# Chunk totals of a gated linear attention: from one-column matmuls to a small DMA, in a new program order

## Chip, cores and metric

One core of a Trainium2 chip. The metric is the device time of one launch in microseconds. Each version is run several times beside the kernel before on the same chip. A profile is one execution; its span is some 2 us shorter than the device time.

## The reference

A gated linear attention (4 batches, 8 heads, 768 steps, head size 48), then a feed-forward layer on its output (384 to 2048 to 384) with the gate `h * cos(h)`.

```python
for t in range(S):
    state = alpha[:, :, t, :, None] * state + np.einsum('bhd,bhe->bhde', k[:, :, t], v[:, :, t])
    y[:, :, t] = np.einsum('bhd,bhde->bhe', q[:, :, t], state)
...
h = x @ w_in
g = h * np.cos(h)
return (g @ w_out).astype(np.float32)
```

## The kernel before

Each sequence is cut into 6 chunks of 128 steps, 24 chunks in all. Per chunk, ScalarE takes the logarithm of alpha; a matmul with a triangle of ones sums it over time (positions on partitions, 8 x 48 = 384 columns); ScalarE takes `exp` of the sum and of its negative. q and k are multiplied by these, so that inside the chunk the attention is a masked product of two matrices. The state passed to the next chunk is scaled by the chunk's total decay. That total is the last row of `exp(cumsum)`, but it is needed down the partitions (one number per row of the state), so it has to be turned from a row into columns.

The kernel before computes it again in the other direction, with one-column matmuls:

```python
def cums(j0, n):                                   # chunks j0 .. j0+n-1, n = 1 or 2
    ...
    for i in range(lo, lo + n):
        nc.tensor.matmul(cum_ps[g][:, i, 0:HD], triu_bf, lnab[:, g % 2, i, :, 0:D], start=True, stop=True)
        for p in range(NP):                        # 4 pairs of heads
            nc.tensor.matmul(cum_ps[g][:, i, HD + p : HD + p + 1],
                lnab[:, g % 2, i, 2 * p : 2 * p + 2].rearrange("s h d -> s (h d)"), ones_bf, ...)

def exps(j0, n):
    ...                                            # icp: exp(-cumsum)
    nc.scalar.activation(out=cp_t[g][:, lo : lo + n], in_=cum_ps[g][:, lo : lo + n, 0:CW], func=AF.Exp, scale=1.0)

def emask(j):                                      # GpSimd: total x block mask, used when the state is scaled
    ...
```

The whole program is a list of small units in a string `ORDER`, run in that order on each engine. `F`, `G` are halves of the first feed-forward product, `V`, `W` of the second, `f_`, `g_` the cosine on ScalarE, `p`, `Q_` the gate on VectorE, `C`/`E` cumsum and exponentials of a pair of chunks, `w3` three dummy matmuls that are meant to keep TensorE's clock up.

## Time and profile before

| | before |
|---|---|
| time, median of the first runs | 192.87 us |
| first feed-forward matmul | 32.9 us after the start |
| from there to the last TensorE work ("the middle") | 154.4 us |
| ScalarE busy | 119.4 us of 190.7 |

The prediction shows the lines. TensorE is the bound; from 33 us on it has no pause to speak of, and before that, waits between engines decide.

### The profile page before, as it was taken

To read this page: it belongs to the slowest core of one execution; us is meant where nothing else is said; L and a number is where in the kernel's file an instruction comes from. 1 tells how busy PE (TensorE), PEld (TensorE's weight loads), DVE (VectorE), ACT (ScalarE), POOL (GpSimd) and SP (SyncE) were. 2 spreads that over 40 slices of the span, in tenths; PEclk is the share of its full clock that TensorE was granted. 3 is DMA by queue.
4 is the path that set the end of the run, shared out by engine and by line. 5 is a ranking of instruction groups with operands and counts; after the bars stand their busy time and mean duration, and the time that the engine had idled before them with its cause. 6 is when DMAs were issued, how large, how long until landed. Compare 5 with 4: busy or idle time off the path is not lost.

```text
span 190.7 us, 5672 instructions
## 1 busy us (share of the span) xinstructions
PE 181.7 (95%) x2410; PEld 138.3 (73%) x2410; DVE 128.3 (67%) x159; ACT 119.4 (63%) x135; POOL 74.8 (39%) x116
## 2 busy tenths in 40 slices
PE   0999999999999999999999999999899999999992
PEld 0345545998766887696987788968669877797761
DVE  6137458999686389649577886885667685578520
ACT  3211448799555859984974999887586363364522
POOL 3422763212923550853961747064450456010000
PEclk9999999999999999999999999999999999999999
DMA  6999999999999989899999779996956798321112
GB/s 129 188 186 187 163 286 364 343 370 213 214 225 225 215 161 228 182 198 194 235 188 170 170 120 194 182 196 142 168 134 140 154 205 168 87 64 24 41 45 83
DMA packets 123225, 34.22 MB, mean 179 GB/s; under 512 B 116544, under 2 KB 121664, under 8 KB 123200
## 3 DMA queue, kind: packets, MB, share of 16 engines
q1 hardware_dynamic: 119744, 29.14, 82.3%
q10 hardware_dynamic: 3456, 4.72, 7.4%
q8 instruction: 19, 0.31, 0.7%
q14 instruction: 6, 0.05, 0.1%
HBM read 25.17 MB, written 4.72 MB: 157 GB/s over the span
## 4 chain that ended last, share of the span: by engine, by line
PE 90%; DMA 5%; DVE 1%; SPq 1%; ACT 1%; issue 0%; DVEq 0%; ACTq 0%
PE t L330 33%; PE o_new L352 31%; PE w_new L368 8%; PE t L235 4%; PE t L218 3%; DMA t<-kqb 3%; PE t L292 2%; PE cum_new L157 2%; PE t L260 2%; PE t L289 2%; PE t L313 2%; DMA a_new<-in_alpha_dram 2%; PE cum_new L161 1%; DVE t L244 1%; SPq L104 1%
## 5 line engine op out<-in xcount | busy, mean ns | idle before, releaser
L330 PE MATMUL t<-x,w 128*128 128x128 bf16 x1152 | 70.4, 219 | 0.0
L352 PE MATMUL o_new<-w,g_new 128*128 128x384 bf16 x384 | 68.8, 326 | 0.0
L344 DVE TENSOR_TENSOR g_new<-t,c_sb 128x1024 bf16<-128x1024 f32 x48 | 57.8, 1218 | 15.0 <-ACT c_sb L338 14.6
L330 PEld LDWEIGHTS <-w 128*128 128x128 bf16 x1152 | 65.6, 98 | 1.5
L338 ACT ACTIVATE c_sb<-t,halfpi 128x1024 bf16<-128x1024 f32 x48 | 52.4, 1113 | 18.8 <-PE t L330 15.9
L352 PEld LDWEIGHTS <-g_new 128*128 128x128 bf16 x384 | 35.4, 98 | 20.2
L185 POOL TENSOR_TENSOR kqb<-t,icp_new 128x384 bf16<-128x384 f32 x24 | 23.9, 999 | 19.0 <-ACT icp_new L175 10.6
L244 DVE TENSOR_TENSOR t<-t,mask_f 128x1024 bf16<-128x1024 f32 x24 | 29.0, 1216 | 3.1 <-PE t L235 3.1
L274 POOL TENSOR_TENSOR ub<-sc,Em 128x384 bf16<-128x384 f32 x16 | 13.3, 830 | 37.8 <-DVE sc L272 36.1
L357 ACT ACTIVATE o_sb<-o_new 128x384 f32<-128x384 f32 x24 | 11.7, 489 | 25.9 <-PE o_new L352 25.9
L191 POOL TENSOR_TENSOR kqb<-t,cp_new 128x384 bf16<-128x384 f32 x22 | 21.9, 1000 | 12.0 <-DMA t<-in_q_dram 10.7
L299 DVE CAST t<-t 128x384 bf16<-128x384 f32 x24 | 13.3, 554 | 12.6 <-PE t L292 12.6
L195 POOL CAST vpb<-t 128x384 bf16<-128x384 f32 x24 | 12.4, 519 | 19.1 <-DMA t<-in_v_dram 16.5
L368 PE MATMUL w_new<-warm 128*128 128x512 bf16 x67 | 19.7, 426 | 0.0
L175 ACT ACTIVATE icp_new<-cum_new 128x768 f32<-128x768 f32 (+1 forms) x13 | 9.8, 758 | 15.4 <-PE cum_new L161 14.8
L224 DVE COPY t<-t 128x1024 bf16<-128x1024 bf16 x13 | 8.9, 688 | 10.0 <-PE t L218 9.9
L144 ACT ACTIVATE lnab<-a_new 128x768 bf16<-128x768 f32 (+1 forms) x13 | 10.3, 795 | 5.4 <-DMA a_new<-in_alpha_dram 4.8
L137 ACT ACT_TABLE_LOAD x9 | 11.5, 1283 | 2.4 <-ACT o_sb L357 1.6
L338 ACT ACT_TABLE_LOAD x9 | 11.5, 1283 | 0.6 <-ACT o_sb L357 0.5
L272 DVE TENSOR_TENSOR sc<-t,ub 128x384 f32<-128x384 f32 x16 | 8.9, 554 | 4.5 <-PE t L260 4.4
L292 PE MATMUL t<-vpb,t 128*128 128x48 bf16 x192 | 11.3, 183 | 0.2 <-DVE t L244 0.2
L157 PE MATMUL cum_new<-lnab,triu_bf 128*128 128x384 bf16 x24 | 7.3, 333 | 4.3 <-ACT lnab L144 4.3
(43 smaller groups left out, 132.0 us busy)
## 6 DMA issues: line engine op xcount, KB each, us to landing
a_new<-in_alpha_dram SPq DMA_DIRECT2D x24, 192.0 KB, 4.6
t<-in_q_dram SPq DMA_DIRECT2D x24, 192.0 KB, 4.4
t<-in_v_dram SPq DMA_DIRECT2D x24, 192.0 KB, 4.5
t<-in_k_dram SPq DMA_DIRECT2D x24, 192.0 KB, 4.8
out_dram<-o_sb ACTq DMA_DIRECT2D x24, 192.0 KB, 3.1
w1f<-in_moe_w_in_dram SPq DMA_DIRECT2D x4, 768.0 KB, 7.9
w2f<-in_moe_w_out_dram SPq DMA_DIRECT2D x4, 768.0 KB, 10.7
t<-kqb SPq DMA_TRANSPOSE x11, 4.0
```

The lines of the kernel that those rows point to most:

```text
L185: nc.gpsimd.tensor_tensor(out=khb[:, j % 3, :, 0:D], in0=k_t.pop(j), in1=icp.rearrange("s (h d) -> s h d", h=H), op=ALU.mult)
L191: eng.tensor_tensor(out=qhb[:, j % 3, :, 0:D], in0=q_t.pop(j), in1=cp[:, 0:HD].rearrange("s (h d) -> s h d", h=H), op=ALU.mult)
L195: nc.gpsimd.tensor_copy(out=vpb[:, j % 3, :, 0:D], in_=v_t.pop(j))
L244: nc.vector.tensor_tensor(out=t.rearrange("s (h t) -> s h t", h=H), in0=A_ps.pop(j).rearrange("s (h t) -> s h t", h=H), in1=mask_f.unsquee ...
L274: eng.tensor_tensor(out=ub[:, us(j), :, 0:96].rearrange("r p (a e) -> r p a e", a=2), in0=sc.rearrange("r p (a e) -> r p a e", a=2), in1=E ...
L292: nc.tensor.matmul(t[:, h * D : (h + 1) * D], A_t[j][:, ACOL[h] * C : (ACOL[h] + 1) * C], vpb[:, j % 3, h], start=first, stop=True, skip_g ...
L299: nc.vector.tensor_copy(out=t, in_=y_ps.pop(j)[:, 0:HD])
L330: nc.tensor.matmul(t[:, f], w1[:, kk, ft * C : (ft + 1) * C], x_t[j][:, kk], start=(kk == 0), stop=(kk == 2))
L338: nc.scalar.activation(out=c_sb, in_=h_ps[j, half], func=AF.Sin, bias=halfpi, scale=1.0)
L344: nc.vector.tensor_tensor(out=g_new, in0=h_ps.pop((j, half)), in1=c_t.pop((j, half)), op=ALU.mult)
L352: nc.tensor.matmul(o_ps[j][:, 0:DM], g[:, f], w2[:, half * HF + f], start=(f == 0 and half == 0), stop=(f == HF - 1 and half == 1))
L368: nc.tensor.matmul(w_ps, warm[:, 0:C], warm, start=True, stop=True)
```

## The change

Its intent: take 96 matmuls from TensorE, the bound, and let the DMA engines turn the row into columns. The exponential is written in another layout, so that the 8 values for one partition stand side by side; two DMAs of 48 rows per pair of chunks spread the last row. The program order was made anew for it.

```diff
-            for p in range(NP):
-                nc.tensor.matmul(
-                    cum_ps[g][:, i, HD + p : HD + p + 1],
-                    lnab[:, g % 2, i, 2 * p : 2 * p + 2].rearrange("s h d -> s (h d)"),
-                    ones_bf, start=True, stop=True,
-                )
...
-            cp_new = cpool.tile([C, 2, CW], FP, tag="cpl")
+            cp_new = cpool.tile([C, 2 * D, 2, NP], FP, tag="cpl")
...
-        nc.scalar.activation(out=cp_t[g][:, lo : lo + n], in_=cum_ps[g][:, lo : lo + n, 0:CW],
-                             func=AF.Exp, scale=1.0)
+        nc.scalar.activation(
+            out=cp_t[g][:, :, lo : lo + n].rearrange("s x i p -> s i p x"),
+            in_=cum_ps[g][:, lo : lo + n, 0:HD].rearrange("s i (p x) -> s i p x", p=NP),
+            func=AF.Exp, scale=1.0)
+        for a in range(2):
+            nc.scalar.dma_start(
+                out=tot[64 * a : 64 * a + D, g % 4, lo : lo + n],
+                in_=cp_t[g][C - 1 : C, a * D : (a + 1) * D, lo : lo + n])
...
     ORDER = (   # all of it replaced
```

In the write of the exponential the innermost index is x, whose step in `cp` is 2 x 4 floats, 32 bytes. The q product reads `cp` with the same step.

## The prediction

> **What bounds the kernel now.** I read the page from the top: busy shares, slices, the chain, then the groups by form, and last the stretches and the timeline.
>
> ```profile
> span 190.7 us, 5672 instructions
> PE 181.7 (95%) x2410; PEld 138.3 (73%) x2410; DVE 128.3 (67%) x159; ACT 119.4 (63%) x135; POOL 74.8 (39%) x116
> ...
> PE   0999999999999999999999999999899999999992
> ...
> PE 90%; DMA 5%; DVE 1%; SPq 1%; ACT 1%; issue 0%; DVEq 0%; ACTq 0%
> ```
>
> TensorE is busy in every slice but the first and the last, and the chain is TensorE for 90%. Busy does not mean useful, though: 67 of its instructions are dummy 512-column matmuls (group L368, 19.7 us) that keep its clock up while the start-up waits for others. So I split the span at the first feed-forward matmul. The chain view has that at 32.97 us and the last TensorE work ending at 187.33. The three stretches:
>
> ```profile
> 0.00:33.00 33.00, 28.15 (x246) 14.03 (x247) 17.90 (x31) 13.13 (x19) 14.35 (x29) 1.00 1.17 213
> 33.00:187.40 154.40, 153.55 (x2166) 124.27 (x2165) 110.44 (x129) 105.81 (x117) 60.43 (x87) 1.00 0.86 174
> 187.40:190.70 3.30, 0.00 (x0) 0.00 (x0) 0.00 (x0) 0.42 (x1) 0.00 (x0) 1.00 0.33 119
> ```
>
> The columns after the length are TensorE, weight loads, VectorE, ScalarE and GpSimd. In the middle TensorE lacks under 1 us of being always busy. Since ends of matmuls are modelled, I check it by start-to-start time: the chain shows 24 feed-forward-1 matmuls in 1.34 us, 8 feed-forward-2 matmuls in 1.30, 8 scores in 0.33, the state in 0.28, outputs in 0.36 (0.22 for a first chunk), eight transposes in 0.45, three in 0.18, cumsum with totals 0.27 per chunk. What stands after the first feed-forward matmul is then 48 x 1.34 + 48 x 1.30 = 126.7, scores 19 x 0.33 = 6.3, outputs 18 x 0.36 + 3 x 0.22 = 7.1, states 16 x 0.28 = 4.5, transposes 8 x 0.45 + 10 x 0.18 = 5.4, cumsums 16 x 0.27 = 4.3: 154.3 us against 154.4 measured. There is no slack to win in the middle. It gets shorter only if TensorE has less to do. The first 33 us are the other place: there waits decide, and dummies fill.
>
> **What the Trainium skill says.** "TensorE: Matmul & The Clock Gate", section "Wait — 56ns, not 53.3ns?", gives a floor of about 25 ns start to start however few columns a matmul has. The trace agrees, and shows what one column costs:
>
> ```profile
> 18.47 0.33 PE L157 MATMUL cum_new<-lnab,triu_bf 128*128 128x384 bf16 x1
> 18.63 0.24 PE L161 MATMUL cum_new<-ones_bf,lnab 128*128 128x1 bf16 x4
> 18.74 0.32 PE L157 MATMUL cum_new<-lnab,triu_bf 128*128 128x384 bf16 x1
> ...
> L161 PE MATMUL cum_new<-ones_bf,lnab 128*128 128x1 bf16 x96 | 5.8, 164 | 0.0
> ```
>
> The four stand between 18.63 and 18.74: 0.11 us per chunk, 27 ns each. The mean of 164 ns in the group's row is latency, and its 5.8 us is not what they cost.
>
> The same page, section "What's actually happening", says that the array starts at half clock and needs some 3.4 us of sustained work. The trace agrees in kind: the first 19 dummies take 6.89 us (0.36 each), later ones 0.215. "GPSIMD Engine Reference", section 7 "Performance pitfalls for Q7 kernels", says that reads with a step over 8 bytes cost about 50% more per element; no row of the kernel before reads so, but the changed one will. [...]the quickest output store of this trace landed in 1.9.
>
> **The change, part by part.** (1) Removed: 96 one-column matmuls, 24 x 0.11 = 2.6 us of TensorE. Eight chunks' worth (0.9 us) lies in the start-up, where dummies and waits absorb it. Sixteen chunks (C4 to C11 in pairs) lie in the middle, where it counts in full: 16 x 0.11 = 1.76 us. (2) Removed: the 0.91 us clearing of lnab on VectorE; nothing at the start waits for it. (3) Removed on GpSimd: eight or nine small Em products (12 of two chunks each instead of 20), 0.22 us each, beside other work.
>
> (4) Added: 26 small DMAs on ScalarE's queue.
>
> ```profile
> L358 ACTq DMA_DIRECT2D out_dram<-o_sb x24: 338/338/406, 49.7 to 187.9; - x24
> L191 POOL TENSOR_TENSOR kqb<-t,cp_new 128x384 bf16<-128x384 f32 x22 | 21.9, 1000 | 12.0 <-DMA t<-in_q_dram 10.7 <-ACT cp_new L177 1.2
> ```
>
> An issue holds that queue 0.34 us, so 26 x 0.34 = 8.8 us, 0.7 per exponential pair. ScalarE goes from 119 to about 128 busy-or-issuing of 190: not the bound. In the start-up, though, each pair of issues stands ahead of the next logarithm. I estimate 0.3 to 0.6 us on the path there. In the middle the tot tile is needed many microseconds after the exponential, so 2 to 4 us of landing are hidden. (5) Changed layout: cp is now written and read with 32-byte steps. If the page's 50% holds, the 22 products of row L191 go from 1.0 to 1.5 us, GpSimd from 75 to about 84 us, 44%: hidden in the middle, and at most one product (0.5 us) on the start-up path. I take the strided exponential as unchanged at 0.81 us; no row shows it.
>
> (6) Moved: the whole order. Before the first feed-forward matmul the new order has 64 dummies (67 before), the same transposes, scores and outputs, and three states instead of four. After it stand the fourth state (+0.28) and 5 dummies (+1.08). So the middle has 154.4 - 1.76 + 0.28 + 1.08 = 154.0 us of work: only 0.4 less.
>
> For the start-up I walked the new order by hand with the durations above (eviction of transposes 0.69, masking 1.21, state sum and output cast 0.56, weight cast 0.68, products 1.0). The loads go out one after another at about 1.0 us as before; the alpha of chunk 0 is now second, so its logarithm starts about 0.6 us later. 9 and 4 cold dummies bring the first transposes to about 11.3 us (11.45 before); the pair of transposes for chunk 1 falls near 15.7, the second cumsum pair near 19, output 0 near 19.5. From there single buffers in PSUM tie TensorE to VectorE: transposes 2 at about 21, state 1 at 23.7, output 1 at 24.9, output 2 at 27.4, transposes 4 at about 28.8 (behind the q and k products on GpSimd), their eviction 30.3, the x copy 31.4, state 2, and the first feed-forward matmul at about 31.8. That is 1.2 us earlier than 32.97, give or take 1.2.
>
> Just after it the order runs three feed-forward halves in a row; the fourth needs the third and fourth quarter of w1, and I find VectorE's last cast ending near 38.5 behind two gates, with TensorE there from about 37.6. I charge 0.4 us for this and for seams like it. The sum: -1.2 (start) - 0.4 (middle) + 0.4 (waits) = -1.2 us on 192.87: about 191.7 us.
>
> **The rivals.** A: the start-up gain is not there. Slower q products and DMA issues ahead of logarithms push the first feed-forward matmul to 33 us or beyond. For it: the chain in the start-up alternates between engines, so each delay adds. Then 193 to 194. B: ScalarE stalls on completion marks. In the built program the eight completion marks of DMAs are used in turn, and 24 of the 26 small DMAs first wait for an earlier DMA to land, as the loads and stores do too. A load held up behind a transpose on SyncE's queue, or a load that now waits for a small DMA, could stop ScalarE and with it the feed-forward buffers. For it: SyncE's queue waits for others 7.6 and 7.3 us in the wait table. Against: the stores had the same waits, and TensorE lost nothing. If it bites several times, 195. C: the new order packs better than I walked, with the first feed-forward matmul at 30 and no later wait: -3 - 0.4, 189.5; a bit more would need an even shorter start. D: the full 2.6 us shows and the dummies cover real waits that vanish: 190.2.
>
> **Range and chances.** Faster by over 2% needs under 189.0, 3.9 us: more than all removed matmuls together, so only the start-up could give it. Slower needs over 196.7, which takes repeated stalls under B. Start-up uncertainty of about 1.5 us and middle waits of -0.4 to +3 give 189.0 to 194.5 for 8 in 10. Chances: faster 0.13, same 0.80, slower 0.07.
>
> **What would show it.** Right: row L161 gone; TensorE busy down some 2 us with 69 dummies; the first feed-forward matmul at 31 to 33 us; q products on GpSimd near 1.5 us; small-DMA issues near 0.34 us each; the middle at 153.5 to 155.5 us. Wrong: first feed-forward matmul before 30.5 or after 34; slices of TensorE below 9 in the middle; long waits of ScalarE's queue for DMAs; exponentials much above 0.81 us.

## More of the kernel before

One more detail matters later: how ScalarE passes through the end of an exponential pair. In the timeline (start, length, engine, line, operation, output and input) of the kernel before:

```profile
63.53 0.81 ACT L177 ACTIVATE cp_new<-cum_new 128x776 f32<-128x776 f32 x1
64.36 1.28 ACT L338 ACT_TABLE_LOAD   x1
65.66 1.11 ACT L338 ACTIVATE c_sb<-t,halfpi 128x1024 bf16<-128x1024 f32 x1
```

The exponential ends, and the switch to the cosine's table begins at once: 0.83 us from the start of the one to the start of the other.

## The result

198.01 us against 192.61 for the kernel before in the same runs: ratio 1.028 (95% interval 1.023 to 1.034). It is slower by more than 2%, and outside the range. (Ratios are the mean of one kernel's fast runs over the mean of the other's in the same rounds, so not quite the quotient of the medians quoted.)

From the page of the kernel after:

```profile
span 196.0 us, 5512 instructions
PE 180.3 (92%) x2312; PEld 136.2 (70%) x2316; DVE 127.1 (65%) x158; ACT 128.1 (65%) x135; POOL 77.1 (39%) x108
...
PE   1996999999998989999999999899899999799993
...
PE 13%; ACT 2%; issue 1%; ACTq 1%; DVE 0%; DVEq 0%
```

TensorE's slices now have 8s and a 7 in the middle. The chain, TensorE for 90% before, can be followed back for 18% of the span only; then it reaches ScalarE's queue, where instructions were issued and no recorded wait is left to follow. The stretch from the first feed-forward matmul (32.15 us) to TensorE's end:

```profile
32.15:192.79 160.64, 154.81 (x2114) 123.43 (x2112) 110.84 (x130) 111.42 (x116) 64.55 (x84) 1.00 0.79 167
```

160.6 us for which 154.0 were predicted, and TensorE idle for 160.64 - 154.81 = 5.8 us of them. The start is near what was predicted (31.8). ScalarE's groups and the record of the tot tile, then the timeline of ScalarE at the end of a pair:

```profile
L169 ACT ACTIVATE cp_new<-cum_new 128x768 f32<-128x768 f32 x11 | 17.3, 1569 | 0.0
L135 ACT ACT_TABLE_LOAD x9 | 11.5, 1283 | 2.4 <-ACT o_sb L354 1.6 <-PEq L427 0.7
L335 ACT ACT_TABLE_LOAD x9 | 11.5, 1283 | 7.3 <-DVE t L241 1.7 <-DVE x L315 1.6 <-POOL kqb L188 1.3
```

```profile
L174 ACTq DMA_DIRECT2D tot<-cp_new x26: 508/588/1232, 7.0 to 161.1; - x26
```

```profile
117.89 1.57 ACT L169 ACTIVATE cp_new<-cum_new 128x768 f32<-128x768 f32 x1
119.49 1.17 ACTq L174 DMA_DIRECT2D tot<-cp_new  x2
120.74 1.28 ACT L335 ACT_TABLE_LOAD   x1 [1.28 <-DVE t L241]
```

The exponential takes 1.57 us, not 0.81; each DMA issue holds ScalarE's queue for 0.59 us (median; minimum and maximum beside it), not 0.34. From the exponential's start to the table load is 2.85 us, against 0.83. The table loads' "idle before" rose from 0.6 to 7.3 us, and the names of its releasers are of no use: those engines had long been done. ScalarE was issuing DMAs, which do not count as busy. So its busy 128 us understate it: 9.1 us of longer exponentials are in it, but not the 26 issues, which fill 16.5 us of the timeline. Here is how that reaches TensorE, late in the run. First come pieces from the beginning of the chain that ended last (start, length, what), then the timeline behind them:

```profile
160.54 0.53 ACTq L174
...
161.10 0.60 ACTq L174
...
161.79 0.08 ACT L335
...
163.09 1.11 ACT c_sb L335
164.20 0.39 ACT o_sb L354
...
164.63 2.76 PE o_new L349 x16
167.39 1.35 PE t L327 x24
```

```profile
168.77 1.11 ACT L335 ACTIVATE c_sb<-t,halfpi 128x1024 bf16<-128x1024 f32 x1 [0.85 <-PE t L327]
...
169.92 1.22 DVE L341 TENSOR_TENSOR g_new<-t,c_sb 128x1024 bf16<-128x1024 f32 x1 [1.35 <-ACT c_sb L335]
...
171.06 0.55 DVE L269 TENSOR_TENSOR sc<-t,ub 128x384 f32<-128x384 f32 x1
...
171.63 0.40 PE L232 MATMUL t<-t 48*128 48x128 bf16 x8 [1.26 <-DVE sc L269]
```

The chain begins at the two DMA issues of the last pair. Behind them stand the table load, a cosine and the copy of an output (`o_sb`); TensorE's second product starts late for that copy (0.30 us), and the first product and the next cosine (168.77) follow it. That late cosine makes the gate late, the gate stands on VectorE ahead of the state sum, and the second of two groups of scores on TensorE waits 1.26 us. In e12 below, with the same order and a shorter hold, the same two groups run in one piece:

```profile
163.47 0.62 PE L231 MATMUL t<-t 48*128 48x128 bf16 x16
```

### The profile page after: what moved, and what is told of

The parts are those of the page before. It is cut to its first block, busy times and chain, and to the rows that moved or that the text cites. A ratio compares the mean times of both kernels' runs of the same rounds, so it can differ in the third digit from the quotient of the medians.

```text
span 196.0 us, 5512 instructions
## 1 busy us (share of the span) xinstructions
PE 180.3 (92%) x2312; PEld 136.2 (70%) x2316; DVE 127.1 (65%) x158; ACT 128.1 (65%) x135; POOL 77.1 (39%) x108
## 5 line engine op out<-in xcount | busy, mean ns | idle before, releaser
L349 PEld LDWEIGHTS <-g_new 128*128 128x128 bf16 x384 | 36.0, 98 | 21.3 <-issue 0.4
L188 POOL TENSOR_TENSOR kqb<-t,cp_new 128x384 bf16<-128x384 f32 x22 | 26.0, 1187 | 12.3 <-DMA t<-in_q_dram 8.0
L365 PE MATMUL w_new<-warm 128*128 128x512 bf16 x65 | 19.2, 420 | 1.4 <-DVE warm L57 1.2
L169 ACT ACTIVATE cp_new<-cum_new 128x768 f32<-128x768 f32 (+1 forms) x13 | 19.0, 1460 | 0.0
L365 PEld LDWEIGHTS <-warm 128*128 128x128 bf16 x69 | 6.6, 105 | 11.5 <-issue 6.6
```

What stands on the lines that cost most here:

```text
L169: nc.scalar.activation(out=cp_t[g][:, :, lo : lo + n].rearrange("s x i p -> s i p x"), in_=cum_ps[g][:, lo : lo + n, 0:HD].rearrange("s i ...
L188: eng.tensor_tensor(out=qhb[:, j % 3, :, 0:D].rearrange("s (p a) d -> s p a d", a=2), in0=q_t.pop(j).rearrange("s (p a) d -> s p a d", a=2 ...
L349: nc.tensor.matmul(o_ps[j][:, 0:DM], g[:, f], w2[:, half * HF + f], start=(f == 0 and half == 0), stop=(f == HF - 1 and half == 1))
L365: nc.tensor.matmul(w_ps, warm[:, 0:C], warm, start=True, stop=True)
```

## The experiments

Theory 1: the changed arithmetic holds ScalarE too long (stepped exponential, DMA issues), and everything behind it in order comes late. Theory 2: the new program order packs TensorE worse by itself. Theory 3: the small DMAs act in another way, by their landing or by the completion marks that they share with the loads.

| version | time, us | ratio (95%) | first ff matmul | middle | TensorE idle in it |
|---|---|---|---|---|---|
| before | 192.2 to 192.6 | 1 | 32.9 | 154.4 | 0.8 |
| after | 198.01 | 1.028 (1.023 to 1.034) | 32.15 | 160.6 | 5.8 |
| order alone | 192.64 | 1.003 (1.001 to 1.004) | 30.2 | 158.1 | 2.8 |
| arithmetic alone | 208.67 | 1.084 (1.079 to 1.090) | 33.3 | 170.5 | 11.4 |
| after, contiguous exponential* | 191.87 | 1.000 (0.996 to 1.005) | 31.75 | 156.7 | 2.8 |
| after, no small DMAs* | 190.76 | 0.991 (0.989 to 0.993) | 31.3 | 155.1 | 2.0 |
| after, neither* | 188.21 | 0.982 (0.977 to 0.986) | 29.4 | 153.5 | 0.4 |
| neither, ScalarE copy of 1.9 us per pair* | 193.38 | 1.005 (1.000 to 1.010) | 31.25 | 157.0 | 2.5 |
| no small DMAs, ScalarE copy of 1.4 us* | 196.60 | 1.021 (1.017 to 1.026) | 32.0 | 159.4 | 5.0 |
| one DMA in place of two | 192.83 | 1.005 (1.000 to 1.009) | 32.1 | 156.6 | 2.9 |
| one DMA, steps moved to the read | 190.42 | 0.989 (0.985 to 0.994) | 30.9 | 154.0 | 0.9 |

Starred versions give a wrong result on purpose. Times are medians of fast runs. The last three columns come from each version's one profile: the start of its first feed-forward matmul, the stretch from there to the end of the last one, and TensorE's idle time in that stretch. (For "order alone" the profile is a second, single run; see below. e6 and e7, which failed, are told in the text.)

### Order alone, arithmetic alone

```diff
 # e1: before, with the new ORDER
-        "E_": emask,
+        "E_": lambda g: (emask(2 * g), emask(2 * g + 1)),
 # e2: after, with the old ORDER; emask again per chunk, from tot
+            out=Em, in0=tot[:, (j // 2) % 4, j % 2].unsqueeze(2).to_broadcast([C, NP, 2]),
```

> The old arithmetic (four one-column matmuls per chunk, no small DMA, contiguous exponential) in the new program order. Theory 1 (ScalarE is made late by the added work: the exponential at 1.57 us in place of 0.81, and 26 DMA issues of 0.59 us): the new order without that work has no long gaps on TensorE; first feed-forward matmul at or before 32 us, time 190 to 193.5 us. Theory 2 (the new order itself packs worse on TensorE, whatever the arithmetic): 196 to 199 us, with the gaps near 62, 72, 124, 138 and 171 us still there.

> The new arithmetic (small DMAs, strided exponential, no one-column matmuls) in the old program order. Theory 1: the same 24 us of extra ScalarE time meet an order that made no room for them: 196 to 201 us. Theory 2: the old order keeps TensorE packed and the removed matmuls show as up to 1.8 us: 190 to 192.5 us.

192.64 and 208.67 us. The order alone is as fast as before (0.3% apart), so theory 2 falls. It starts the feed-forward part at 30.2 us, 2.7 us earlier than before, and its middle is 3.7 us longer in the single run that was profiled. The new arithmetic in the old order is slower by 8%, more than the 196 to 201 us that theory 1 gave: in the new order the same arithmetic costs 10.7 us less (208.67 - 198.01). But not all of that loss need be ScalarE's. In the old order GpSimd's product with the totals (`Em`) stands close behind the exponentials, and GpSimd stood there for the small DMAs to land:

```profile
POOL Em L197 <- DMA tot<-cp_new: 28.2, 8, 7.3
```

That is 28.2 us in 8 waits, against 9.1 us in two in the kernel after. So the landing, which the prediction called hidden, shows on GpSimd in another order; what it cost TensorE there, no run separates. In that profile the granted clock was 0.973 as well, so a little of the loss is clock.

The first profile of the order-only kernel fell in an execution at half the TensorE speed: 370.85 us, with TensorE 97% busy and the first feed-forward product 141.9 us in its group's row in place of 70.4. (The granted clock that the record gives for it is 1.00 all the same.) Its three timed runs were normal. The profile was taken again:

> The order-only kernel again, for a profile at full clock: the first one fell in a run at half the TensorE speed (370.85 us). Expected: 192 to 193 us, no idle time of TensorE over 0.5 us after the first feed-forward matmul, ScalarE busy near 119 us.

```profile
30.24:188.30 158.06, 155.31 (x2178) 124.46 (x2176) 111.64 (x130) 107.95 (x117) 62.88 (x94) 1.00 0.87 176
```

193.7 us in a single run. Idle 158.06 - 155.31 = 2.8 us, more than the hoped-for none (waits for transposing DMAs, of 1.2 and 1.1 us in all, are among it).

### Each cost taken away

```diff
 # e3: exponential contiguous, the same two DMAs from a contiguous row (totals misplaced)
-            out=cp_t[g][:, :, lo : lo + n].rearrange("s x i p -> s i p x"),
-            in_=cum_ps[g][:, lo : lo + n, 0:HD].rearrange("s i (p x) -> s i p x", p=NP),
+            out=cp_t[g][:, lo : lo + n],
+            in_=cum_ps[g][:, lo : lo + n, 0:HD],
 # e4: no DMAs (totals zero)
-        for a in range(2):
-            nc.scalar.dma_start(out=tot[...], in_=cp_t[g][...])
 # e5: both
```

> The changed kernel with the exponential written contiguously and the row taken by the same two DMAs of the same size; the totals then stand in the wrong places, so the result is wrong on purpose. Exponential back at 0.81 us, q product on GpSimd back at 1.00 us, DMA issues unchanged near 0.59 us. If the strided exponential (8.4 us of ScalarE) is the larger part of theory 1: 193 to 195 us. If the DMA issues are: 196.5 to 198 us. Theory 2: 197.5 to 198.5 us.

> The changed kernel without the 26 small DMAs; the totals stay zero, so the result is wrong on purpose; strided exponential kept at 1.57 us. If the issues and the waits before them (15 us and more of ScalarE's queue) are the larger part: 192 to 194.5 us. If the strided exponential is: 196 to 197.5 us. Theory 2: 197.5 to 198.5 us.

> The changed kernel with neither cost: contiguous exponential, no small DMAs, totals zero (wrong on purpose). Theory 1a (the two costs are one debt of ScalarE's queue with a threshold: paying back either is nearly enough): 189 to 191 us, hardly under the 190.8 of the kernel without the DMAs. Theory 1b (each costs 6 to 7 us of its own): about 186 us.

191.87, 190.76 and 188.21 us, with relative errors of 0.37, 0.17 and 0.17. In the contiguous one the exponential took 0.80 us, the q product 1.00, the issues 0.59 as before; so e3 and e5 take away the stepped q product too (e12 below keeps it). Both e3 and e4 came out under all the ranges given for them. Taking away either cost gives back 6 to 7 us of the 9.8 between "after" and "neither"; the second then gives only 2.6 to 3.7. So the two are one debt, as theory 1a said, though not so sharply: 188.2 is lower than it expected. The middle without both:

```profile
29.39:182.87 153.48, 153.13 (x2115) 122.89 (x2112) 111.60 (x130) 106.95 (x116) 61.24 (x84) 1.00 0.84 178
```

153.5 us, TensorE packed. The prediction's 154.0 us of TensorE work was right: with neither cost this order makes a 188 us kernel.

### ScalarE held, without any DMA

```diff
 # e13: e5, and after each exponential pair
+        nc.scalar.activation(out=pad[:, 0 : 2 + n],
+            in_=warm.unsqueeze(1).to_broadcast([C, 2 + n, 512]), func=AF.Copy)
 # e14: after without the DMAs, stepped exponential kept, and in the DMAs' place
+        nc.scalar.activation(out=pad,
+            in_=warm[:, 0:470].unsqueeze(1).to_broadcast([C, 3, 470]), func=AF.Copy)
```

> The kernel with neither cost (188.2 us, wrong on purpose) plus one meaningless ScalarE copy after each exponential pair, 1536 or 2048 elements, estimated 1.5 to 1.9 us, about the time that the strided write and the two DMA issues take of the queue. If occupying ScalarE at that place is the whole cause: 196 to 200 us. If the small DMAs act otherwise too (landing, completion marks, the row's traffic): 189 to 193 us.

> The changed kernel (strided exponential kept) with each pair of small DMAs replaced by one meaningless ScalarE copy of 1410 elements, estimated 1.38 us, so that ScalarE is held as long as in the changed kernel (2.85 us from the start of the exponential to the next instruction) but no small DMA exists; totals zero, wrong on purpose. If holding ScalarE is the whole cause and the last 3 us of holding cost more than the first 24: 197 to 199 us. If the small DMAs cost some microseconds in another way (landing, completion marks, loads behind them): 193 to 195 us.

The first gave 193.38 us, between what the two theories expected. It holds ScalarE 1.8 us per pair, the changed kernel 2.0. The second was made to hold it nearly as long as the changed kernel. Its timeline:

```profile
116.84 1.58 ACT L170 ACTIVATE cp_new<-cum_new 128x768 f32<-128x768 f32 x1
118.17 1.42 ACT L174 ACTIVATE pad<-warm 128x1410 bf16<-128x1410 bf16 x1
119.61 1.28 ACT L334 ACT_TABLE_LOAD   x1
```

2.77 us from the exponential to the table load (2.85 in the changed kernel), no small DMA at all. The middle of the version without DMAs (e4), and of the same with the copy (e14):

```profile
31.30:186.43 155.13, 153.14 (x2114) 123.05 (x2112) 111.06 (x130) 111.13 (x115) 64.62 (x84) 1.00 0.80 172
31.99:191.40 159.41, 154.43 (x2115) 123.26 (x2112) 111.11 (x130) 120.23 (x124) 64.61 (x84) 1.00 0.85 169
```

These two differ by the copy alone, and TensorE's idle time goes from 2.0 to 5.0 us. The time goes from 190.76 to 196.60 us, 5.8 of the 7.3 us that separate e4 from the changed kernel. 196.60 us is a little under the 197 to 199 that full explanation called for, well above the 193 to 195 of theory 3. In ratios, holding ScalarE explains 1.021 - 0.982 = 0.039 of the 1.028 - 0.982 = 0.046 between "neither" and "after", some 84% (with the stepped q product in it). The two intervals (1.017 to 1.026, and 1.023 to 1.034) touch, so whether the last 1.4 us are an effect of the DMAs themselves stays open. One trace of an effect of the DMAs is in the waits of SyncE's queue in the kernel after:

```profile
SPq L109 <- DMA tot<-cp_new: 4.9, 1, 4.9
```

The load of the last quarter of w1 was issued 4.9 us late, after a wait for a small DMA. It did no harm that shows: TensorE pauses 0.27 us for a cast of w1 there, but it pauses 0.28 us at the same place in the versions without small DMAs (e4, e5, e14).

Between the two pads the time rises by 3.2 us, though the hold per pair rises only from 1.8 to 1.95 us. The second also has the stepped q products, and no run separates the two, so it is not shown that the cost of holding is steeper at its end.

### Other places for the same work

```diff
 # e6: the DMAs from SyncE's queue
-            nc.scalar.dma_start(
+            nc.sync.dma_start(
 # e7: contiguous exponential, GpSimd makes the stepped layout of the last 32 rows, ScalarE issues
+        nc.gpsimd.tensor_copy(out=rw[96:128, :, 0:n].rearrange("s x i p -> s i p x"),
+            in_=cp_t[g][96:128, lo : lo + n].rearrange("s i (p x) -> s i p x", p=NP))
```

> The changed kernel, the small DMAs issued from SyncE's queue in the same place of the order, strided exponential kept; correct. If the holding of ScalarE's queue is the cost: 190.5 to 192.5 us, near the kernel without the DMAs. If the landing of the small DMAs or the shared completion marks are (they are kept here, and loads now stand behind the small DMAs): 195 us or more.

> Contiguous exponential; GpSimd copies the last 32 rows into the transposed layout (768 elements, estimated 1.2 to 1.8 us, 13 times), and the two DMAs go from there, still issued by ScalarE; correct. ScalarE's queue must now wait for GpSimd before it issues. Theory 1 in its simple form (busy time of ScalarE): 191.5 to 193 us like the wrong contiguous kernel. If ScalarE stopping for GpSimd costs more than the stride saved: 195 us or more.

239.25 us (ratio 1.245) and, in e7's two fast runs, 217.30 and 214.49 us (ratio 1.124; two more were slow). Both lie in the worse branch of what was expected, and far beyond its 195 us. The granted clock was 0.91 to 0.93 in e6 and 0.976 to 0.984 in e7, so a part is clock. The waits say why, the first line from SyncE's queue in e6, the second from GpSimd in e7:

```profile
SPq L174 <- ACT cp_new L169: 46.0, 12, 9.4
```

```profile
POOL rw L174 <- ACT cp_new L169: 23.8, 11, 6.1
```

SyncE stood 46 us at the small DMAs, waiting for exponentials, and all loads and DMA transposes behind them were late. In e7, GpSimd stood 24 us for the exponentials, with the k, q and v work of later chunks behind it, and ScalarE then waited for GpSimd. The work was cheap in both places. Its wait, in an in-order queue full of other work, was not. These runs do not bear on theory 1 as they were meant to: they bring in a larger cost of their own.

### The two costs made smaller

```diff
 # e8b: heads padded to 64 rows, one DMA of 128 rows per pair
+    cpa = consts.tile([C, 4, 2, 64, 2, NP], FP, tag="cpa")
+        nc.scalar.dma_start(out=tot[:, g % 4, lo : lo + n],
+            in_=cp_t[g][C - 1 : C, :, :, lo : lo + n].rearrange("s a x i p -> s (a x) i p"))
 # e12: e8b, the same elements in another order
-            out=cp_t[g][:, :, 0:D, lo : lo + n].rearrange("s a x i p -> s i p a x"),
-            in_=cum_ps[g][:, lo : lo + n, 0:HD].rearrange("s i (p a x) -> s i p a x", p=NP, a=2),
+            out=cp_t[g][:, :, 0:D, lo : lo + n],
+            in_=cum_ps[g][:, lo : lo + n, 0:HD].rearrange("s i (p a x) -> s a x i p", p=NP, a=2),
```

> The two DMAs of 48 rows made one of 128 rows (padding rows included), strided exponential kept; correct. If a queue is held per DMA near 0.59 us, half of 15 us comes back: 193 to 195.5 us. If it is held per row sent, the one DMA takes 1.2 us or more and the time stays 196.5 to 199.

> The one-DMA kernel with the same exponential taken in another order of elements: the writes to SBUF run in 32-byte blocks without gaps, the reads from PSUM step 384 bytes instead. Correct. If the cost of 0.76 us per pair comes from the stepped writes, the exponential is back near 0.81 us and the time falls from 192.8 to 189.5 to 191.5 us. If any step (also of reads) costs as much, the exponential stays at 1.5 us or more and the time at 192 to 194 us.

192.83 us with one DMA, just under the range of the better branch: the queue is held per DMA, not per row (477 ns for 128 rows, 588 for 48). 190.42 us with the steps moved to the PSUM side. Both give the right result. (A contiguous exponential with one DMA of single elements did not build.) The tile's records and the middle in e12:

```profile
L170 ACT ACTIVATE cpa<-cum_new x13: 484/804/807, 6.0 to 152.9; 128x768 f32<-128x768 f32 x11, 128x384 f32<-128x384 f32 x2
L174 ACTq DMA_DIRECT2D tot<-cpa x13: 477/478/522, 6.5 to 153.8; - x13
L187 POOL TENSOR_TENSOR kqb<-t,cpa x22: 1182/1187/1194, 16.7 to 154.9; 128x384 bf16<-128x384 f32 x22
...
30.87:184.86 153.99, 153.07 (x2114) 122.90 (x2112) 110.97 (x130) 105.78 (x115) 64.56 (x84) 1.00 0.81 174
```

The exponential is back at 0.804 us though its reads now step 384 bytes in PSUM: it was the stepped write that cost. The q products are still stepped in e12 (1187 ns, as in the kernel after), so the 2.4 us between the two versions are the exponential's alone. The Trainium skill, "SBUF — State Buffer", section "Door 1: The DMA port swizzle", says that SBUF has lines of 16 bytes and that an access which moves to a new line each time pays. The trace agrees for ScalarE's writes (1.57 against 0.80 us for the same 768 elements). This version beats both kernels: 1.1% faster than before (0.985 to 0.994), with a middle of 154.0 us. Its runs spread from 188.9 to 191.5 us.

## Why the prediction was wrong

- **Bound and work: right.** TensorE bounds the kernel, and the middle holds 154.0 us of work by the prediction; with the two costs gone it took 153.5, in e12 154.0.
- **Start: right in sum, by luck: two errors cancelled.** 31.8 predicted, 32.15 measured. The order alone starts at 30.2, so it gained 2.7 us and not 1.2, and the arithmetic took back 1.9, where 0.3 to 0.6 for the issues and at most 0.5 for the products were foreseen. On VectorE, which makes the first two q products, the step was not considered at all: 852 ns against 553 contiguous (e3).
- **Step 5 failed: "I take the strided exponential as unchanged at 0.81 us; no row shows it."** It is 1.57 us, 9.1 us over the run. Its warning sign was in the same step: a penalty for 32-byte steps was taken over for GpSimd's reads and not considered for ScalarE's writes. GpSimd's own penalty was smaller than the 50% (1.19 us, +19%), and in the middle it did no harm: e12 keeps it and has 154.0 us there.
- **Step 4 failed in size: "An issue holds that queue 0.34 us".** That was the store's figure. The small DMAs hold it for 0.59 us each, and 16.5 us of the timeline go to them in place of 8.8.
- **The inference failed that joined them: "not the bound", so hidden in the middle.** The sum was made over the span (128 of 190 us). But these 2 us come in one piece, 13 times; eight of these are in the middle, five of them directly ahead of a table load and the cosines that TensorE's PSUM buffers wait for. Three experiments carry this: either cost removed gives 6 to 7 us back, and a meaningless copy in the same place brings most of the loss back. No run held ScalarE as long in smaller pieces or at another place, so that the one piece and its place matter, and not the sum, is argued from the chain and not shown by a run.
- **Rival B had the right victim and the wrong weapon.** ScalarE stalled by holding and not by waiting for completion marks: all 13 pairs of small DMAs start within 0.1 us of the end of their exponential, and with no small DMA at all the time was 196.6. Rival A's part, a start eaten by slower products and issues, was seen (1.9 us) but hidden by a better order. Rivals C and D did not come; e5 shows what C would have been, 188.2 us.
- **"Against: the stores had the same waits, and TensorE lost nothing"** was a fair argument about marks and no argument about time held.

## What to carry to other kernels

When work is moved off the bounding engine, write down for the receiving queue how long it is held in one piece and what stands behind it, DMA issues included, since no busy share shows them. An engine at 65% can still set the pace if the piece stands ahead of what the bound waits for. Take a duration from a row with the same access pattern and the same kind of DMA, or call it unknown; here two borrowed figures hid some 17 us of ScalarE's time, and putting the steps on the read side with one DMA for two turned a loss of 2.8% into a gain of 1.1%.

## What the Trainium skill lacked or had wrong

- "ScalarE: Activation LUTs", section "What ACT_TABLE_LOAD costs", gives one element per cycle per lane at 1.2 GHz for every function. For writes with 32-byte steps to SBUF the runs show (1569 - 862) / 384 = 1.84 ns per element, against (806 - 484) / 384 = 0.84 contiguous (e5). The page has no figure for steps.
- "SBUF — State Buffer" says in the section cited above that non-contiguous PSUM access slows matmuls; it has nothing on ScalarE's reads from PSUM. With 384-byte steps these cost nothing here: 804 ns for 768 elements, against 804 to 806 contiguous.
- "GPSIMD Engine Reference", section "7. Performance pitfalls for Q7 kernels", has +50% for stepped reads. A product with one of its two inputs stepped by 32 bytes took 1187 ns against 1000, +19%.
- "DMA: Bandwidth & Descriptors" gives 512 sequencer cycles per copy for earlier generations, in section "Why a DMA increments its semaphore by 16 and not by 1"; it does not say how this depends on the transfer or on the issuing engine. For ScalarE's queue the runs show 338 ns for a store of 192 KB, 588 (508 at least) for 48 rows of 32 bytes from SBUF to SBUF, 478 for 128 such rows.
- "TensorE: Matmul & The Clock Gate", section "What's actually happening", describes half clock as the state after idling, and its section "Seeing it yourself" knows of a clock stuck at a quarter for 50 us and more. One execution of the order-only kernel ran at half speed through its 368.9 us while TensorE was 97% busy, and its record gives the granted clock as 1.00. Its cause was not found.
